# Two sigmoids of a pair of groups placed ahead of the squares of their step, in the other order

## The chip, the cores and the metric

The kernel runs on one core of one Trainium2 chip. The metric is the device time of one execution in microseconds. The core has five engines that run their own instruction streams in order and meet only through semaphores: PE (matrix multiply; its weight loads are listed as PEld), DVE (vector), ACT (activation functions), POOL (GpSimd) and SP, which here only issues DMA transfers. Matmul results land in PSUM banks; everything else lives in SBUF tiles.

## The reference: what is computed

Two layers follow each other on x of shape 4 x 12608 x 128, all in float32.

The first is an attention through 32 inducing vectors. For each of the four batches, the 32 vectors attend to all 12608 tokens (stage A below), and the tokens then attend to the 32 results (stage B below):

```
h = mab(I, x)          # softmax(scale * I x^T) x   : 32 x 128 per batch
y = mab(x, h)          # softmax(scale * x h^T) h   : 12608 x 128 per batch
```

The second is a gated channel mix of each token with its predecessor:

```
xk = mu_k * y + (1 - mu_k) * y_prev
xr = mu_r * y + (1 - mu_r) * y_prev
k  = relu(xk @ w_k)              # 1024 wide
v  = (k * k) @ w_v
out = sigmoid(xr @ w_r) * v
```

## The kernel before, in words

**Groups, units, steps.** The tokens of a batch are cut into 24 groups of 512 tokens and one of 320 (`NG` = 25). A group's 1024 hidden channels are four *units* of 256 channels (`NU` = 4). The main loop (L1047) runs over steps n, one unit per step, 400 units for the four batches, so a step is one quarter of a group.

**What a step does.** At every even n, `up` (L795) issues on PE the up-projection L803 of two units into the two buffers of `ps_a`. Then `square` (L806) turns one unit's result into its square: DVE rectifies it into `k_t` (L813); ACT squares `k_t` into `kh`, rounded to the matmul's input format (L818), and squares `k_t` again in place in full precision (L820); POOL subtracts the two into the rounding rest `kl` (L823). In some steps (`high_vector`, L1016 to L1021) DVE makes `kh` instead (L815); the in-place square on ACT then waits for it, because it overwrites what DVE reads. Four steps later (`LAG` = 4), `down` (L825) multiplies `kh` and `kl` by the split w_v (L831) and accumulates a group's output in one of two PSUM banks `ps_v`. `gate` (L834) multiplies it by the sigmoid `rT`, and `store` transposes it and sends it out on SP's queue.

**The gate's sigmoid.** The matmuls for two groups, 2k and 2k+1, are issued together on PE by `zpair` (L858), at steps n = 8k+6, from k = 1 on: 49 pairs. They are three pairs of matmuls at L781. One group's result goes to the `ps_v` bank that `down` of group 2k+1 will fill two steps later; the other's goes to a bank borrowed from the attention, `pb_a` or `pb_b`. `pb_a` is stage A's bank, for its scores (L372) and its accumulation (L441); `pb_b` is stage B's, for its scores (L620). The borrowed bank becomes free when ACT has read it with the sigmoid (L786), and what the attention issues on PE next into that bank waits for this. `zpair` returns a function that emits the two sigmoids, in the order of the groups: first the one in `ps_v` (the earlier group), then the one in the borrowed bank. The loop calls it after the step's squares. For the last pair of all, `pb_b` takes the place of `ps_v`. Groups 0 and 1 have their sigmoid from `zgate`, which is not touched.

**The attention between.** Stage A of the next batch and stage B of this one are cut into small pieces that are put into the loop at given steps: `at(n, f)` places one at the end of step n, `soon(n, f)` before the squares of step n (the exponentials of both stages, L409 and L637, go there). The exponential and the sigmoid need different activation tables, so ACT loads a table (listed under the line of the instruction that needs it, L786, L408 or L637) whenever it goes from one to the other; the squares, copies and casts need no load.

**Order.** The program is written in the order in which each engine executes it (`manual_schedule`); the semaphore waits follow from which tile is read and written. Nothing is planned from costs. On SP's queue stand, in program order, the transfers of stage A's transposed input (`xt`, L347), of stage B's results into the tiles `R` that the up-projection and the gate read (L587, L600, doubled onto the other half of the partitions by L594), the inputs' loads (L207) and the stores (L854). A buffer of `R` is refilled only after the gate matmuls L781 of the group that used it.

Of the kernel before, what the change touches and what calls it, by code (L numbers as in the profile page):

```python
# [19 lines left out]
def kernel(  # L20
# [46 lines left out]
    def pv_tile(side=None):  # L67

        return pv.tile([P, G], F32, name=f"ps_v{next(sides) if side is None else side % 2}")

    def pb_tile(bank=None):

        return pb.tile([P, G], F32, name="pb_" + (bank or next(banks)))
# [784 lines left out]
    def zpair(n, two):  # L858

        last = two[1].b == B - 1 and two[1].g == NG - 1  # L860
        r = n - (0 if n >= UB else 4)
        spot = r % UB
        side = "b" if r < (B - 1) * UB and SEG <= spot < 7 * SEG and spot % SEG == 2 else "a"
        ps = [pb_tile("b") if last else pv_tile(two[1].b * NG + two[1].g), pb_tile(side)]
        ps = [t[:, :grp.w] for grp, t in zip(two, ps)]
        for m, (a, k) in enumerate(TERMS):
            for h in range(2):
                two[h].zpart(ps[h], a, k, slice(HP * h, HP * (h + 1)), m)
        return lambda: run([lambda grp=grp, t=t: grp.sigmoid(t) for grp, t in zip(two, ps)])

    def run(th):
        for f in th:
            f()
# [68 lines left out]
    def head():  # L942


        last = NBLK - 1
        ab[0].tr()
        warm(8)
        ab[1].tr()
        ab[0].scores()
        for k in range(NBLK):  # L950
            ab[k].maxi()
            ab[k].expo()
            place(PARTS[k][0])
            if k > 0:
                ab[k - 1].hmm()
            if k == last:
                maxes()
            if k > 0:
                ab[k - 1].acc()
                ab[k - 1].sums()  # L960
            if k == 0:
                constants()
            if k + 2 < NBLK:
                ab[k + 2].tr()
            if k == last:
                ab[k].sums()
                weights()
                spin(3)
            ab[k].etrans()
            place(PARTS[k][1])  # L970
            ab[k].ecopy()
            if k < last:
                ab[k + 1].scores()
        gate = weights_sum()
        held = sm.tile([P, 1], F32, name="held", bufs=1)
        nc.gpsimd.tensor_copy(out=held, in_=gate[:, 0:1])
        for c in range(FC // cg):
            split_wv(c)
        spin(3)
        ab[last].hmm()  # L980
        ab[last].acc()
        load_x(1, 0)
        hfin()
        assert not work
# [10 lines left out]
    def start():  # L995

        wk = wpart(0, pv_tile)
        wg = wpart(1, pv_tile)
        (sc0, df0, ex0, nm0, turn0, hi0, lo0, idle), *rest = [stage_b_first(g) for g in range(Q)]
        run([sc0, wk[0], rest[0][0], df0, ex0, wk[1], nm0, lambda: idle(1), turn0, hi0, wk[2], lo0])  # L1000
        plan = ((None, None, None, at, soon, soon, at), (at,) * 4 + (soon, soon, at), (at, at, soon, at, soon, soon, at))
        steps = ((0, 0, 0, 0, 2, 2, 2), (0, 1, 1, 2, 4, 4, 4), (4, 5, 6, 7, 8, 8, 8))
        for fs, when, ns in zip(rest, plan, steps):
            for k, (f, put, n) in enumerate(zip(fs, when, ns)):
                if put is not None:
                    put(n, f)
                elif k > 0:
                    f()
        at(0, wg[0])
        at(0, wg[1])  # L1010
        at(1, wg[2])
        soon(3, lambda: units[0][0].zgate())
        soon(7, lambda: units[NU][0].zgate())
# [3 lines left out]
    for b in range(B):  # L1017
        t = b * UB + (4 if b == 0 else 0)
# [14 lines left out]
    for b in range(B):  # L1033
        for g in range(NG):
            grp = Group(b, g)
# [8 lines left out]
    with tc.manual_schedule():  # L1044
        head()
        start()
        for n in range(len(units) + LAG + 2):  # L1047
            grp, u = units[n] if n < len(units) else (None, n % NU)
            old, ou = units[n - LAG] if LAG <= n < len(units) + LAG else (None, 0)
            for grp_ in gates.pop(n, []):  # L1050
                grp_.gate()
            if grp is None:
                run(late)
                late = []
            else:
                if n % 2 == 0:
                    for g, v in units[n:n + 2]:
                        g.up(v)
                sig = None
                if n % (2 * NU) == NU + 2 and n > 2 * NU:  # L1060
                    sig = zpair(n, (units[n - NU - 2][0], units[n - 2][0]))
                run(early.pop(n, []))
                whole = n in (end - 3, end - 1, end)
                low = grp.square(u, n in high_vector, whole)
                run(late)
                late = [low] if whole else []
                if not whole:
                    low()
                if sig:
                    sig()  # L1070
            for grp_ in stores.pop(n, []):
                grp_.store()
            if old is not None:
                old.down(ou)
            run(events.pop(n, []))
# [30 lines left out]
```

## Time and profile before

| what | value |
|---|---|
| median of 3 runs | 1184.02 us (1182.8 to 1186.4) |
| the profiled execution | 1180.83 us, its span 1179.0 us |
| busy in the span: PE, DVE, ACT, POOL | 92%, 77%, 82%, 80% |
| mean granted clock of PE | 0.983 |
| one square on ACT (L818, L820), mean | 1041 and 1050 ns |
| one sigmoid of 128x512 (L786), mean | 584 ns |
| one activation table load | 1283 ns |
| one subtraction on POOL (L823), mean | 2379 ns |

How to read the lines that follow: a line of the timeline gives the start in us from the beginning of the span, the duration, the engine, the source line, the operation and its tiles, then in brackets how long the engine stood idle before it and what ended that. A line of waits gives who waited for whom, the total in us, how often, and the longest. A busy PE includes modelled ends of its matmuls.

### The profile page before, as it was taken

The numbers are of one execution on the slowest core, as the hardware profiler recorded it, in microseconds if no ns is written. First come the engines' busy times: TensorE is split into PE (matmuls) and PEld (weight loads), VectorE is DVE, ScalarE is ACT, GpSimd is POOL, SyncE is SP. The second block draws the span as 40 slices with busy tenths as digits, with TensorE's granted clock in tenths as the row PEclk, the third lists the DMA queues.
The fourth block names the chain that finished last, engine by engine and source line by source line (L and its number), as shares of the span: only waits on it lengthen the run. The fifth ranks groups of instructions, "written<-read, shape, count | busy, mean of one in ns | idle before, by whom it ended". The sixth has DMA issues, their size and how long they took to land.

```text
span 1179.0 us, 19549 instructions
## 1 busy us (share of the span) xinstructions
PE 1089.9 (92%) x6722; PEld 739.2 (63%) x6722; DVE 904.3 (77%) x1296; ACT 966.5 (82%) x1101; POOL 945.1 (80%) x419
## 2 busy tenths in 40 slices
PE   7799999989999998999999999898989899999998
PEld 5456566656666665666656656556665666666676
DVE  5798788876778887887778788877757677878665
ACT  6497788777898888777989878878678989999996
POOL 2278878878879887777879978877777899999996
PEclk9999999989999999999999999999999999999999
DMA  9215646456155564656326636565422444344431
GB/s 280 89 28 117 154 105 153 99 126 140 29 110 129 126 134 116 143 131 127 61 42 122 151 91 144 117 139 134 83 47 36 89 96 90 63 92 79 81 66 33
DMA packets 267634, 123.61 MB, mean 105 GB/s; under 512 B 225648, under 2 KB 247056, under 8 KB 265232
## 3 DMA queue, kind: packets, MB, share of 16 engines
q1 hardware_dynamic: 267200, 122.35, 47.7%
q8 instruction: 53, 0.87, 0.3%
q14 instruction: 45, 0.37, 0.1%
q10 hardware_dynamic: 336, 0.02, 0.0%
HBM read 28.07 MB, written 25.82 MB: 46 GB/s over the span
## 4 chain that ended last, share of the span: by engine, by line
PE 44%; DVE 21%; ACT 19%; issue 8%; SPq 4%; DMA 3%; DVEq 0%; ACTq 0%
PE ps_v L831 23%; PE ps_a L803 14%; DVE k_t L813 11%; ACT kh L818 5%; ACT k_t L820 5%; ACT rT L786 3%; ACT L786 2%; PE pb_a L372 2%; DVE ot L847 1%; PE pb_b L620 1%; PE pb_a L441 1%; DVE kh L815 1%; SPq L854 1%; DVE oT L836 1%; DMA out_dram<-ot 1%
## 5 line engine op out<-in xcount | busy, mean ns | idle before, releaser
L823 POOL TENSOR_TENSOR kl<-k_t,kh 128x1024 fp32r<-128x1024 f32 (+1 forms) x397 | 933.4, 2379 | 189.5 <-ACT k_t L820 160.7
L813 DVE TENSOR_SCALAR k_t<-ps_a 128x1024 f32<-128x1024 f32 (+1 forms) x400 | 475.1, 1197 | 142.9 <-PE ps_a L803 134.4
L818 ACT ACTIVATE kh<-k_t 128x1024 fp32r<-128x1024 f32 (+1 forms) x352 | 366.3, 1041 | 119.7 <-DVE k_t L813 118.4
L820 ACT ACTIVATE k_t<-k_t 128x1024 f32<-128x1024 f32 (+1 forms) x397 | 416.4, 1050 | 55.9 <-DVE kh L815 23.6
L803 PE MATMUL ps_a<-R,W 64*128 64x512 f32 (+1 forms) x2400 | 343.2, 416 | 7.9 <-DVE k_t L813 6.5
L803 PEld LDWEIGHTS ps_a<-R,W 64*128 64x128 f32 x2400 | 212.9, 189 | 137.9 <-issue 50.0
L831 PE MATMUL ps_v<-kh,wvh 128*128 128x512 f32 (+1 forms) x800 | 273.3, 423 | 8.4 <-ACT rT L786 8.2
L831 PE MATMUL ps_v<-kh,wvl 128*128 128x512 f32 (+1 forms) x800 | 249.1, 393 | 0.0
L831 PE MATMUL ps_v<-kl,wvh 128*128 128x512 f32 (+1 forms) x800 | 248.6, 392 | 0.0
L831 PEld LDWEIGHTS ps_v<-kh,wvh 128*128 128x128 f32 x800 | 134.2, 189 | 102.2 <-issue 62.1
L831 PEld LDWEIGHTS ps_v<-kh,wvl 128*128 128x128 f32 x800 | 150.7, 189 | 35.1
L831 PEld LDWEIGHTS ps_v<-kl,wvh 128*128 128x128 f32 x800 | 149.7, 188 | 34.9
L836 DVE TENSOR_TENSOR oT<-ps_v,rT 128x512 f32<-128x512 f32 (+1 forms) x100 | 66.8, 668 | 6.9 <-PE ps_v L831 6.2
L847 DVE STREAM_TRANSPOSE ot<-oT 128x512 f32<-128x512 f32 x96 | 66.8, 696 | 0.0
L815 DVE SCALAR_TENSOR_TENSOR kh<-ps_a,k_t 128x1024 fp32r<-128x1024 f32 x48 | 58.8, 1225 | 2.5
L344 DVE STREAM_TRANSPOSE xs<-xb 128x512 f32<-128x512 f32 x72 | 50.0, 695 | 0.9 <-issue 0.4
L375 DVE TENSOR_REDUCE mx<-pb_a 128x1 f32<-128x512 f32 x18 | 12.5, 692 | 44.6 <-PE pb_a L372 44.6
L781 PE MATMUL ps_v<-R,Wg 64*128 64x512 f32 (+1 forms) x150 | 45.4, 404 | 0.0
L372 PE MATMUL pb_a<-xt,indT 128*32 128x512 f32 x144 | 26.7, 670 | 18.0 <-ACT rT L786 15.4
L786 ACT ACT_TABLE_LOAD x31 | 39.8, 1283 | 0.6
L781 PE MATMUL pb_a<-R,Wg 64*128 64x512 f32 (+1 forms) x120 | 36.3, 410 | 2.3 <-ACT e1t L409 2.3
L441 PE MATMUL pb_a<-xb,e 128*32 128x128 f32 x576 | 20.2, 282 | 15.7 <-ACT rT L786 15.7
(222 smaller groups left out, 645.4 us busy)
## 6 DMA issues: line engine op xcount, KB each, us to landing
out_dram<-ot SPq DMA_DIRECT2D x184, 128.0 KB, 2.8
R<-R SPq DMA_DIRECT2D x88, 256.0 KB, 3.0
xb<-in_x_dram SPq DMA_DIRECT2D x18, 1024.0 KB, 5.4
xt<-xs SPq DMA_DIRECT2D x288, 64.0 KB, 2.0
R<-hl SPq DMA_DIRECT2D x96, 128.0 KB, 2.3
R<-hl SPq DMA_DIRECT2D x96, 127.8 KB, 2.4
kh<-in_x_dram SPq DMA_DIRECT2D x4, 512.0 KB, 7.7
kl<-in_x_dram SPq DMA_DIRECT2D x4, 512.0 KB, 7.4
```

Of the source, the lines that this page charges most:

```text
L372: nc.tensor.matmul(out=ps[M * i:M * (i + 1), :], lhsT=indT, rhs=S.xt[j, i], start=True, stop=True)
L781: nc.tensor.matmul(out=ps, lhsT=self.S.Wg[a][rows, :], rhs=self.S.R[self.g][rows, k, :self.w], start=(n == 0), stop=(n == len(TERMS) - 1))
L786: nc.scalar.activation(out=self.rT, in_=ps, func=AF.Sigmoid)
L803: nc.tensor.matmul(out=ps[:, r, :w], lhsT=S.W[a][rows, u * P:(u + 1) * P], rhs=R[rows, k, :w], start=(n == 0), stop=(n == 2))
L813: nc.vector.tensor_scalar(out=k, in0=ps, scalar1=0.0, scalar2=None, op0=ALU.max)
L815: nc.vector.scalar_tensor_tensor(out=kh, in0=ps, scalar=0.0, in1=k, op0=ALU.max, op1=ALU.mult)
L818: nc.scalar.activation(out=kh, in_=k, func=AF.Square)
L820: nc.scalar.activation(out=k2, in_=k, func=AF.Square)
L823: return lambda: eng.tensor_tensor(out=kl, in0=k2, in1=kh.bitcast(F32), op=ALU.subtract)
L831: nc.tensor.matmul(out=self.v, lhsT=wt[:, fc, :], rhs=kk[:, c, :], start=(fc == 0 and n == 0), stop=(fc == FC - 1 and n == 2))
L836: nc.vector.tensor_tensor(out=self.oT, in0=self.v, in1=self.rT, op=ALU.mult)
L847: nc.vector.transpose(out=ot[:, o:o + w], in_=self.oT)
```

## The change

Two places are edited. In the loop, the call that emits the two sigmoids moves from behind the step's squares (and behind POOL's subtraction) to in front of them; it stays behind the early pieces, so behind the exponentials of that step. In `zpair`, the two sigmoids swap places: the one in the borrowed bank comes first. The names of the two `rT` buffers swap with them. PE's instructions and their order, DVE's, POOL's and the transfers are as before.

```diff
@@ zpair
-        return lambda: run([lambda grp=grp, t=t: grp.sigmoid(t) for grp, t in zip(two, ps)])
+        return lambda: run([lambda grp=grp, t=t: grp.sigmoid(t) for grp, t in zip(two[::-1], ps[::-1])])
@@ the loop over steps
                 run(early.pop(n, []))
+                if sig:
+                    sig()
                 whole = n in (end - 3, end - 1, end)
                 low = grp.square(u, n in high_vector, whole)
                 run(late)
                 late = [low] if whole else []
                 if not whole:
                     low()
-                if sig:
-                    sig()
```

## The prediction

> **What bounds the kernel now.** I read the page's head first, then who waited for whom, then the timeline around single pair steps, then the DMA queue beside them.
>
> ```profile
> span 1179.0 us, 19549 instructions
> PE 1089.9 (92%) x6722; PEld 739.2 (63%) x6722; DVE 904.3 (77%) x1296; ACT 966.5 (82%) x1101; POOL 945.1 (80%) x419
> ```
> ```profile
> POOL kl L823 <- ACT k_t L820: 160.7, 122, 10.7
> DVE k_t L813 <- PE ps_a L803: 134.4, 90, 6.2
> PEld ps_a L803 <- DVE k_t L813: 20.1, 37, 1.8
> PE pb_a L441 <- ACT rT L786: 15.7, 9, 2.9
> PE pb_a L372 <- ACT rT L786: 15.4, 8, 2.6
> PE ps_v L831 <- ACT rT L786: 8.2, 8, 1.9
> PE pb_b L620 <- ACT rT L786: 8.2, 7, 1.3
> PE pb_a L372 <- DMA R<-R: 2.5, 1, 2.5
> PE pb_a L556 <- ACT rT L786: 2.2, 1, 2.2
> ```
>
> The profiled execution took 1180.83 us, 1.8 outside its span; the median of the runs is 1184.02, 3.2 above it, and I put the change onto that median. PE is the fullest engine, and the others trail it: POOL waits for ACT's squares, DVE's rectifier L813 waits for PE's up-projection L803. PE itself has only 89 us idle, and 49.7 of them (15.7 + 15.4 + 8.2 + 8.2 + 2.2) end with a sigmoid, L786, that was the last reader of a PSUM bank. The wait of 2.5 us put down to a DMA is one more: its weight load names L786. So some 52 us of PE, the engine the others wait for, hang on how late ACT reaches two sigmoids.
>
> **The change, part by part.** No instruction is added or taken away on any engine: 98 sigmoids, their table loads, all DMAs and PE's order stay. On ACT, two sigmoids (with a table load, where an exponential came in between) pass in front of one or two squares, L818 and L820, of their step. What they need, the six L781 matmuls, is issued before that step's squares anyway. The swap inside the pair lets the bank that stage A or B wants go first.
>
> *Stage A's scores, L372, inputs long there.*
>
> ```profile
> 161.48 1.06 ACT L820 ACTIVATE k_t<-k_t 128x1024 f32<-128x1024 f32 x1
> 161.70 0.39 PE L781 MATMUL pb_a<-R,Wg 64*128 64x512 f32 x1
> 164.16 1.06 ACT L820 ACTIVATE k_t<-k_t 128x1024 f32<-128x1024 f32 x1 [1.62 <-DVE kh L815]
> 165.24 1.28 ACT L786 ACT_TABLE_LOAD   x1
> 167.03 0.59 ACT L786 ACTIVATE rT<-pb_a 128x512 f32<-128x512 f32 x1
> 167.67 1.43 PE L372 MATMUL pb_a<-xt,indT 128*32 128x512 f32 x8 [2.58 <-ACT rT L786]
> ```
>
> ACT stood idle 1.62 us before the square. In the new order the load starts when the square of the step before ends, 162.54, and the pb_a sigmoid ends at 162.54 + 1.28 + 0.6 = 164.45; its matmuls ended at 162.09. PE is free at 167.67 - 2.58 = 165.09, so the whole 2.58 goes, with 0.6 to spare. The square itself moves only from 164.16 to about 164.9: most of the 2.4 us that pass it go into ACT's idle time. Four of these sites behave otherwise (next), so of 15.4 + 2.5 there remain 15.4 - 9.5 + 2.5 = **8.4 us**.
>
> *Stage A's scores behind a late transfer.*
>
> ```profile
> 234.17 0.67 SPq L587 DMA_DIRECT2D R<-hl  x1
> 236.25 2.44 SPq L347 DMA_DIRECT2D xt<-xs  x4
> 239.88 0.63 PE L372 MATMUL pb_a<-xt,indT 128*32 128x512 f32 x3 [2.58 <-ACT rT L786]
> 839.90 2.44 SPq L347 DMA_DIRECT2D xt<-xs  x4
> 842.61 1.92 PE L372 MATMUL pb_a<-xt,indT 128*32 128x512 f32 x7 [1.80 <-ACT rT L786]
> ```
> ```profile
> xt<-xs SPq DMA_DIRECT2D x288, 64.0 KB, 2.0
> ```
>
> At four sites (first and last shown; three like the first, 3 x 2.58 + 1.80 = 9.5 us of wait) the last four transfers of xt stand on SP's in-order queue behind L587, which waits for the L781 matmuls of this very step. The fourth is issued near 236.25 + 1.85 = 238.1 and lands 2.0 later, 240.1: at the moment the sigmoid now releases PE. The earlier sigmoid therefore lets three of four score tiles run, and the fourth keeps PE. I take 2.5 us over the four (the fourth tile alone takes about 1.0 from its landing to the next block, against 1.8 from 239.88 now), with 0 and 9.5 as ends.
>
> *Stage A's accumulation, L441.*
>
> ```profile
> 189.46 0.61 ACT L637 ACTIVATE s<-s 128x512 f32<-128x512 f32 x1
> 189.98 1.05 ACT L820 ACTIVATE k_t<-k_t 128x1024 f32<-128x1024 f32 x1
> 192.83 0.59 ACT L786 ACTIVATE rT<-pb_a 128x512 f32<-128x512 f32 x1
> 193.48 1.08 PE L441 MATMUL pb_a<-xb,e 128*32 128x128 f32 x32 [2.01 <-ACT rT L786]
> ```
>
> New: load at 190.07, pb_a done at 190.07 + 1.28 + 0.6 + 0.03 = 191.98, L441 at 192.03 and 1.45 earlier; 0.56 of the wait stays. Nine sites keep at most 9 x 0.56 = 5.0 of 15.7; two have a wait of only 0.3 and keep nothing, two pass two squares: I keep 3.2, gain **12.5** (10.7 to 15.7).
>
> *Stage B's scores, L620.*
>
> ```profile
> 210.94 1.06 ACT L820 ACTIVATE k_t<-k_t 128x1024 f32<-128x1024 f32 x1
> 215.33 0.59 ACT L786 ACTIVATE rT<-pb_b 128x512 f32<-128x512 f32 x1
> 215.97 1.06 PE L620 MATMUL pb_b<-xt,hT 128*32 128x512 f32 x8 [1.35 <-ACT rT L786]
> ```
>
> No load, two squares passed: pb_b is done at 212.0 + 0.6 = 212.6, PE free at 214.62. All seven go: **8.2**; L556 likewise **2.2**. The down-projection L831 waits for the other bank, now second of the two: two squares of 1.06 come behind it and one sigmoid (about 0.5) ahead, 1.6 earlier against a longest wait of 1.9: **7.8** of 8.2 (5 to 8.2).
>
> *PE's clock.*
>
> ```profile
> 167.67 1.43 PE pb_a L372 x8
> 169.10 2.86 PE ps_a L803 x12
> 194.56 1.59 PE ps_a L803 x12
> 203.74 1.12 PE pb_a L372 x8
> ```
> ```profile
> 167.50:171.00 3.50, 3.33 (x18) 2.06 (x20) 0.90 (x2) 2.61 (x4) 1.15 (x2) 0.69 0.00 0
> 193.30:196.80 3.50, 3.32 (x47) 2.49 (x48) 1.24 (x2) 1.07 (x2) 3.41 (x2) 1.00 1.14 208
> ```
>
> After the 2.58 us wait the granted clock is 0.69 over 3.5 us and two blocks take (1.43 - 1.12) + (2.86 - 1.59) = 1.6 us longer; after 2.01 it stayed at 1.00. Such dips stand behind eight of the waits above; five lie at sites whose wait shrinks under 0.6 (167, 444, 693, 792, 867 us), three at the transfer-bound ones. I count 5 x 1.6 = **8.0** (0 to 12.8). The Trainium skill (TensorE: Matmul & The Clock Gate, Part 1: The HAM clock gate) has the clock halved after an idle window of about 3.4 us, free-running; by it, stalls of 2 to 2.9 us need not cost a dip, and the term would be 0 and the time 1146. The row shows the dip after less than a full window, and the row decides.
>
> *What becomes late.* The squares.
>
> ```profile
> 189.63 7.22 POOL L823 TENSOR_TENSOR kl<-k_t,kh 128x1024 fp32r<-128x1024 f32 x3 [1.98 <-PE ps_v L831]
> 199.12 2.42 POOL L823 TENSOR_TENSOR kl<-k_t,kh 128x1024 fp32r<-128x1024 f32 x1 [2.27 <-ACT k_t L820]
> ```
> ```profile
> 1000.00:1100.00 100.00, 98.74 (x539) 68.18 (x540) 84.06 (x102) 92.14 (x98) 94.25 (x40) 1.00 0.41 80
> ```
>
> At the L441 site the square moves from 189.98 to 192.4, and POOL's second subtraction from 192.03 (189.63 + 7.22/3) to 193.4: 1.4 late. POOL's third ends at 198.3 instead of 196.85, still before the 199.12 at which it waits today, and that step's down-projection comes four steps later. So the queue of four steps and POOL's 160.7 us of waiting hide it. Where the cover is thin, in the last batch (window of 1000 us: columns PE, weight load, DVE, ACT, POOL; POOL 94.25 of 100), about 1.1 us of POOL's idle time falls to each pair of 20 us. If it fails there, 13 pairs cost up to 13 x 1.08 = 14; I take 4, nearer to the covered rows.
>
> **Sum:** 8.4 + 2.5 + 12.5 + 8.2 + 2.2 + 7.8 + 8.0 - 4 = **45.6 us**. 1180.8 - 45.6 = 1135.2 for a profiled execution, 1184.0 - 45.6 = **1138** for the median.
>
> **The rivals.** *DVE becomes the bound.* DVE waits for PE 134.4 us, which speaks against; but in the mixed stretches its pieces of both stages lie back to back, and PE catching up eats that slack. Price: each of the 49 pairs brings one wait for L813 of today's mean, 20.1/37 = 0.54 us, 26 us: 1184 - 19 = 1164.
>
> *The transfers are late at the other score sites too*, since SP's queue is tied to PE's gate matmuls: 8.4 and three dips (4.8) are lost: 1151. Against it: at 167 us all transfers had long landed.
>
> *Slower: the squares bind through POOL.*
>
> ```profile
> L786 ACT ACT_TABLE_LOAD x31 | 39.8, 1283 | 0.6
> ```
>
> Each pair's squares come 1.08 us later (two sigmoids), and 1.28 more where a load goes with them, 29 of the 31 loads. If POOL's subtraction sets when k_t buffers come free for L813 and when L831 can run, 49 x 1.08 + 29 x 1.28 = 90 us come in against 50 of gain: 1184 + 40 = 1224. It decides as soon as POOL's lateness outlasts the 2.27 us it waits today before the next step; at 1.4 it doesn't.
>
> *It doesn't do what it says:* PE's waits stay because something else releases PE at the same moment everywhere, as the transfers do at four sites: 1184.
>
> **Chances.** Forecast 0.58, no clock term 0.05, DVE 0.17, transfers 0.06, nothing 0.05, squares 0.09. The forecast's own range is 1119 (upper ends: 3.2 + 7 + 0.4 + 4.8 + 4 = 19.4 us more) to 1163 (lower ends: 1.8 + 2.5 + 2.8 + 8 + 10 = 25.1 less); to hold eight in ten it must reach past DVE's 1164: **1119 to 1166**, leaving out the last two cases. 0.3% is about what a measurement can tell here. Faster 0.58 + 0.05 + 0.17 + 0.06 = 0.86, same 0.05, slower 0.09.
>
> **What would show it.** PE's waits for L786 fall from 49.7 to some 5 to 10 us; L620, L556 and L831 vanish from that list, L441 keeps waits near 0.56 five times. At four sites L372 still has a gap, now with xt transfers as releaser. The granted clock's mean rises from 0.983. POOL's wait for L820 shrinks by roughly the time gained, and its busy time stays. Wrong if new waits PE L803 <- DVE L813 of tens of us appear, if L831 begins to wait for POOL L823, or if the four transfer sites lose their gap altogether.

## The result, and the profile after

The changed kernel takes 1131.12 us (median of 4 runs, 1131.11 to 1134.28). The kernel before, run beside it, took 1183.41 (1182.67 to 1186.4). The ratio is 0.956 with a 95% interval of 0.9537 to 0.9584: 52.3 us less, against 45.6 forecast and a predicted 1138.

The head of the page after:

```profile
span 1129.1 us, 19547 instructions
PE 1083.1 (96%) x6722; PEld 733.4 (65%) x6722; DVE 903.1 (80%) x1296; ACT 963.3 (85%) x1101; POOL 944.8 (84%) x419
```

The profiled execution took 1131.12 us. Its span is 49.9 us shorter than that of the kernel before, and PE's two parts of it are: its idle time fell from 1179.0 - 1089.9 = 89.1 to 1129.1 - 1083.1 = 46.0 us (43.1 less), and its busy time by 6.8. PE's and DVE's instructions come in the same order as before; only ACT's order differs, with the same 31 table loads.

The list of waits after, those that answer to the lines shown of before (who waited for whom, total in us, times, longest):

```profile
POOL kl L823 <- ACT k_t L820: 120.6, 108, 10.7
DVE k_t L813 <- PE ps_a L803: 98.3, 86, 3.3
DVE k_t L813 <- POOL kl L823: 8.0, 11, 2.4
PE ps_a L803 <- DVE k_t L813: 7.9, 14, 1.4
PE pb_a L352 <- ACT e1t L409: 7.8, 3, 2.8
PE pb_a L441 <- ACT rT L786: 3.1, 6, 0.6
PE pb_a L372 <- DMA xt<-xs: 2.3, 2, 1.2
PE pb_a L372 <- ACT k_t L820: 2.0, 2, 1.0
PE ps_v L831 <- ACT rT L786: 0.6, 1, 0.6
```

Of 52.2 us of PE waiting that ended with a sigmoid L786 (the 2.5 put down to a DMA counted in), 3.1 + 0.6 = 3.7 are left, and the mean granted clock rose from 0.983 to 0.995. L620 and L556 are gone from the list. The two lines for L372 are new: the four score sites with a late transfer. Two of the four are put down to the square L820; the experiment on the transfers below shows that it is not what they wait for. POOL's wait for the square fell by 40 us while its busy time stayed, so POOL's slack is what paid for the time gained.

The site at 167 us before, now 5 us earlier (timeline, with ACT, PE and POOL):

```profile
158.80 1.06 ACT L820 ACTIVATE k_t<-k_t 128x1024 f32<-128x1024 f32 x1
159.88 1.28 ACT L786 ACT_TABLE_LOAD   x1
161.18 0.60 ACT L786 ACTIVATE rT<-pb_a 128x512 f32<-128x512 f32 x1
161.67 0.59 ACT L786 ACTIVATE rT<-ps_v 128x512 f32<-128x512 f32 x1
162.15 1.06 ACT L820 ACTIVATE k_t<-k_t 128x1024 f32<-128x1024 f32 x1
162.36 1.07 PE L372 MATMUL pb_a<-xt,indT 128*32 128x512 f32 x8
163.28 2.41 POOL L823 TENSOR_TENSOR kl<-k_t,kh 128x1024 fp32r<-128x1024 f32 x1 [0.33 <-ACT k_t L820]
```

Table load and both sigmoids now stand in front of the square. L372 starts without a gap and takes 1.07 us instead of 1.43. The square runs beside it, and POOL waits 0.33 us for it.

The site at 240 us before, now with the transfer as its limit (PE, ACT and SP's queue):

```profile
226.12 0.60 ACT L786 ACTIVATE rT<-pb_a 128x512 f32<-128x512 f32 x1
226.32 2.44 SPq L347 DMA_DIRECT2D xt<-xs  x4
228.38 2.91 PE L372 MATMUL pb_a<-xt,indT 128*32 128x512 f32 x8 [1.02 <-DMA xt<-xs]
231.22 1.67 PE L803 MATMUL ps_a<-R,W 64*128 64x512 f32 x12
```

The bank is free at 226.12 + 0.60 = 226.72, PE has nothing else to do from 228.38 - 1.02 = 227.36, and still it stands until 228.38. Then the block takes 2.91 us instead of some 1.07; that further parts of xt land only while it runs is tested below. Such a stretched block counts as busy, so the 4.3 us in the list of waits are not all that these transfers cost. Two more blocks are stretched with no gap in front of them: 2.47 us at 266.97 and 2.22 us at 426.05.

### The profile page after: what moved, and what is told of

Its sections match the earlier page's. It is cut to its first block, busy times and chain, and to the rows that moved or that the text cites. A ratio compares the mean times of both kernels' runs of the same rounds, so it can differ in the third digit from the quotient of the medians.

```text
span 1129.1 us, 19547 instructions
## 1 busy us (share of the span) xinstructions
PE 1083.1 (96%) x6722; PEld 733.4 (65%) x6722; DVE 903.1 (80%) x1296; ACT 963.3 (85%) x1101; POOL 944.8 (84%) x419
## 4 chain that ended last, share of the span: by engine, by line
PE 64%; DVE 14%; ACT 11%; issue 4%; SPq 3%; DMA 2%; POOL 1%; DVEq 0%; ACTq 0%; POOLq 0%
PE ps_v L831 35%; PE ps_a L803 20%; DVE k_t L813 7%; ACT kh L818 3%; ACT k_t L820 3%; PE pb_a L372 3%; PE ps_v L781 2%; PE pb_b L620 1%; PE pb_a L441 1%; ACT L786 1%; DVE oT L836 1%; DVE xs L344 1%; DVE ot L847 1%; SPq L100 1%; SPq L193 1%
## 5 line engine op out<-in xcount | busy, mean ns | idle before, releaser
L823 POOL TENSOR_TENSOR kl<-k_t,kh 128x1024 fp32r<-128x1024 f32 (+1 forms) x397 | 933.2, 2385 | 140.0 <-ACT k_t L820 120.6
L813 DVE TENSOR_SCALAR k_t<-ps_a 128x1024 f32<-128x1024 f32 (+1 forms) x400 | 475.7, 1197 | 108.4 <-PE ps_a L803 98.3
L820 ACT ACTIVATE k_t<-k_t 128x1024 f32<-128x1024 f32 (+1 forms) x397 | 415.7, 1050 | 37.9 <-DVE kh L815 5.6
L803 PE MATMUL ps_a<-R,W 64*128 64x512 f32 (+1 forms) x2400 | 337.6, 410 | 9.5 <-DVE k_t L813 7.9
L803 PEld LDWEIGHTS ps_a<-R,W 64*128 64x128 f32 x2400 | 209.1, 186 | 135.5 <-issue 49.2
L831 PE MATMUL ps_v<-kh,wvh 128*128 128x512 f32 (+1 forms) x800 | 272.0, 422 | 0.6 <-ACT rT L786 0.6
L831 PE MATMUL ps_v<-kh,wvl 128*128 128x512 f32 (+1 forms) x800 | 249.0, 393 | 0.0
L831 PE MATMUL ps_v<-kl,wvh 128*128 128x512 f32 (+1 forms) x800 | 248.6, 392 | 0.0
L831 PEld LDWEIGHTS ps_v<-kh,wvh 128*128 128x128 f32 x800 | 133.6, 189 | 92.4 <-issue 58.1
L831 PEld LDWEIGHTS ps_v<-kh,wvl 128*128 128x128 f32 x800 | 150.2, 189 | 34.7
L831 PEld LDWEIGHTS ps_v<-kl,wvh 128*128 128x128 f32 x800 | 149.8, 188 | 34.9 <-POOL kl L823 0.2
L375 DVE TENSOR_REDUCE mx<-pb_a 128x1 f32<-128x512 f32 x18 | 12.5, 692 | 32.9 <-PE pb_a L372 32.9
L372 PE MATMUL pb_a<-xt,indT 128*32 128x512 f32 x144 | 29.1, 604 | 4.2 <-DMA xt<-xs 2.3
L781 PEld LDWEIGHTS ps_v<-R,Wg 64*128 64x128 f32 x150 | 27.8, 190 | 5.9 <-issue 0.5
```

The source lines that it names most:

```text
L372: nc.tensor.matmul(out=ps[M * i:M * (i + 1), :], lhsT=indT, rhs=S.xt[j, i], start=True, stop=True)
L781: nc.tensor.matmul(out=ps, lhsT=self.S.Wg[a][rows, :], rhs=self.S.R[self.g][rows, k, :self.w], start=(n == 0), stop=(n == len(TERMS) - 1))
L803: nc.tensor.matmul(out=ps[:, r, :w], lhsT=S.W[a][rows, u * P:(u + 1) * P], rhs=R[rows, k, :w], start=(n == 0), stop=(n == 2))
L813: nc.vector.tensor_scalar(out=k, in0=ps, scalar1=0.0, scalar2=None, op0=ALU.max)
L820: nc.scalar.activation(out=k2, in_=k, func=AF.Square)
L823: return lambda: eng.tensor_tensor(out=kl, in0=k2, in1=kh.bitcast(F32), op=ALU.subtract)
```

## The experiments

Each ratio is to runs of the kernel before on the same chip. The two halves of the change, the earlier transfers in the kernel after and the late squares ran beside one set of them (median 1185.88); the earlier transfers in the kernel before, the last batch and the first filling beside another (1184.54); the second filling beside a third (1185.09).

**Which half of the change carries it.** First the moved call with the old order inside the pair, as an edit of the kernel after:

```diff
-        return lambda: run([lambda grp=grp, t=t: grp.sigmoid(t) for grp, t in zip(two[::-1], ps[::-1])])
+        return lambda: run([lambda grp=grp, t=t: grp.sigmoid(t) for grp, t in zip(two, ps)])
```

> The changed kernel (1131.1 us) with the old order inside the pair: both sigmoids ahead of the squares, the one in ps_v first. My theory (PE waits for banks, ACT's place in the order sets how long): the borrowed bank is read one sigmoid, about 0.5 us, later. L372 at sites without a late transfer has 0.6 us to spare and stays free; the five waits of L441 go from 0.56 to about 1.06, two others grow by up to 0.5, so PE's waits of L441 rise from 3.1 to about 6.5 us, and the time to 1134 to 1135. Rival, the order inside the pair carries much of the gain: 1145 or more. Rival, it carries nothing: 1131.

Measured: 1136.32 us, ratio 0.9597 (0.9565 to 0.9629), 1 to 2 us more than expected; PE's wait at L441 is 6.6 us, as expected. Then the swap inside the pair alone, as an edit of the kernel before (the same two lines, the other way round):

> The kernel before (1183.4 us) with only the order inside the pair changed; the sigmoids stay behind the squares. My theory: the borrowed bank comes free 0.5 us earlier, so L372, L441 and L620 win about 0.5 us at each of 25 waits (12 us), the waits of L831 for the other bank grow by 0.5 us each (4 us at eight sites, some new ones), and some clock dips go as waits fall from 2.6 to 2.1 us (up to 5 us): 1170 to 1177. Rival, the order carries much of the gain: 1160 or less. Rival, nothing: 1183.

Measured: 1173.63 us, ratio 0.9904 (0.9872 to 0.9936), as expected. The position carries some 49.6 us and the order alone 12.3 (1185.88 less each). Together they are not 62 but 52, since both shorten the same waits: with the position changed, only some 5 us are left for the order. The intervals of the two ratios, 0.956 and 0.9597, overlap by a little; the order's share on top of the position rests as much on the trace, where L441 waits 3.1 us instead of 6.6. The list of waits with the order alone shows what it trades:

```profile
PE ps_v L831 <- ACT rT L786: 12.8, 10, 2.4
PE pb_a L441 <- ACT rT L786: 12.8, 9, 2.4
PE pb_a L372 <- ACT rT L786: 11.7, 6, 2.1
PE pb_b L620 <- ACT rT L786: 4.8, 7, 0.9
```

Each attention bank comes about half a microsecond earlier, and the down-projection's bank that much later: L831 waits 12.8 us instead of 8.2.

**Whether the transfers are the limit at the four sites.** In the kernel after, stage A's last transposition is placed one step earlier, so that its four transfers go onto SP's queue ahead of L587:

```diff
-            at(t + ((1, 2, 3, 7) if b > 1 or j > 1 else (-1, 0, 1, 3) if j else (4, 5, 6, 7))[c], lambda c=c: btr(c))
+            at(t + ((1, 2, 3, 6) if b > 1 or j > 1 else (-1, 0, 1, 3) if j else (4, 5, 6, 7))[c], lambda c=c: btr(c))
```

> The changed kernel with the last of stage A's four transposes one step earlier (7 becomes 6 in its list of steps), so that its four transfers of xt stand on SP's queue ahead of the refill that waits for the gate matmuls. My theory (at four sites L372 now waits for these transfers: its block takes 2.9 us from a start that is already 1.0 late, against 1.07): about 2.8 us come back at each of the four and 1 to 1.4 us at two more whose block takes 2.2 and 2.5 us, so 10 to 14 us: 1117 to 1121, and L372 blocks of 1.07 everywhere. Rival, the gap there is caused by ACT (one view names the square L820 as releaser): 1131.

Measured: 1117.44 us (1116.5 to 1119.06), ratio 0.9436 (0.9406 to 0.9466), as expected. This beats both kernels. SP's queue and PE at the same site:

```profile
220.67 3.07 SPq L347 DMA_DIRECT2D xt<-xs  x4
224.57 0.63 SPq L587 DMA_DIRECT2D R<-hl  x1
227.62 1.07 PE L372 MATMUL pb_a<-xt,indT 128*32 128x512 f32 x8
```

The transfers now stand ahead of L587 and no longer wait for the gate matmuls with it. The groups of instructions (busy us, mean ns of one, idle us before) give the price, first after, then with this edit:

```profile
L372 PE MATMUL pb_a<-xt,indT 128*32 128x512 f32 x144 | 29.1, 604 | 4.2 <-DMA xt<-xs 2.3 <-ACT k_t L820 2.0
```
```profile
L372 PE MATMUL pb_a<-xt,indT 128*32 128x512 f32 x144 | 19.2, 605 | 0.0
```

4.2 us of waiting and 9.9 of stretched blocks go, 14.1 in all: at the four sites with a gap, and some 2.5 of it at the two stretched blocks without one. All 18 blocks now take 1.07 us. The time falls by 1131.1 - 1117.4 = 13.7 between the medians, which were taken in different sets of runs, and by 12.0 between the two profiled spans, since PE waits 2.5 us more at L803 and L534 there.

The same edit in the kernel before:

> The kernel before (1183.4 us) with only the last of stage A's four transposes one step earlier (7 becomes 6). My theory: at the four sites the sigmoid ends at about the moment the last transfer lands, so removing the transfer alone gains only what it keeps inside the block of L372 (0.4 to 0.9 us at four or five sites): 1180 to 1183. If the transfers had been the cause of those waits before, 4 x 2.5 us and their clock dips would go: 1168 or less.

Measured: 1185.97 us over 10 runs, ratio 1.0012 (0.9998 to 1.0026): not even the little that was expected. There L372 still waits for the sigmoid, and the long block is now the clock's doing, which was 0.50 from 239.78 on:

```profile
239.91 2.25 PE L372 MATMUL pb_a<-xt,indT 128*32 128x512 f32 x8 [2.56 <-ACT rT L786]
```

So some 12 to 14 us hang on the transfers only once the sigmoid is early. Taking one of two limits away that end together brings nothing; that is why the transfers did not show in the waits of before.

**What late squares cost.** In the kernel after, two more sigmoids of the same size, whose results nobody reads, come behind the real two and ahead of the squares. Nothing of the computation is left out.

```diff
+        def both():
+            for grp, t in zip(two[::-1], ps[::-1]):
+                grp.sigmoid(t)
+            for grp in two[::-1]:
+                junk = mp.tile([P, G], F32, name="junk", bufs=1)[:, :grp.w]
+                nc.scalar.activation(out=junk, in_=grp.rT, func=AF.Sigmoid)
+        return both
```

> The changed kernel with two more sigmoids of the same size behind each pair's two, from rT into a tile nobody reads: the banks come free as early as before, but the squares of each of the 49 pair steps come about 1.08 us later still. My theory (PE sets the pace, POOL's waiting and the four steps between squares and down-projection hide late squares): between 0 and 10 us, 1131 to 1141, most of it in the last batch. Rival, squares bind through POOL: 49 x 1.08 = 53 us, 1184.

Measured: 1147.39 us, ratio 0.9695 (0.9659 to 0.9732): 16 us more than after, outside what my theory gave and far under the 53 of the rival. Waits that grew:

```profile
POOL kl L823 <- ACT k_t L820: 147.4, 102, 10.7
DVE k_t L813 <- POOL kl L823: 40.0, 43, 3.5
PE ps_a L803 <- DVE k_t L813: 11.9, 15, 2.0
```

The chain that the slower rival described does exist: a late square makes POOL late (147.4 instead of 120.6), POOL holds `k_t` buffers that DVE's L813 needs (40.0 instead of 8.0, 43 times instead of 11), and PE waits more for DVE. It is not shown to be the whole price. PE's idle time grew by 11.7 us, from 46.0 to 57.7; 4.0 of them stand in the last line and 1.1 in new waits of L831 for POOL, and the rest is spread over small waits. The added sigmoids also give ACT 50 us more to do (1013.6 us busy instead of 963.3), and this run does not part that from the lateness. Together they cost 16 of the 49 x 1.08 = 53 us that were added. The change itself adds no work to ACT and stays inside the cover; a second delay of the same size, with its work, does not.

The change for the last batch alone, where I had feared for the cover, is the other side of it. It is an edit of the kernel before: the pairs of steps from 300 on are swapped and emitted ahead of the squares.

```diff
+        o = -1 if n >= 3 * UB else 1
+        return lambda: run([lambda grp=grp, t=t: grp.sigmoid(t) for grp, t in zip(two[::o], ps[::o])])
...
+                if sig and n >= 3 * UB:
+                    sig()
+                    sig = None
```

> The kernel before with the change made only for the pairs of the last batch (steps from 300 on), where no stage A runs and POOL is 94% busy. It separates the price of late squares where the cover is thinnest (prediction: 4 us, at most 14) from the waits of L831 that go there (4.3 us in five waits). My theory: 1179 to 1184, gain and price nearly cancel. Rival, late squares bind through POOL there: 1190 or more. Rival, they cost nothing: 1179.

Measured: 1180.63 us over 10 runs, ratio 0.9964 (0.9951 to 0.9976), so 2.8 to 5.8 us faster. PE's waits at L831 behind 860 us, before and here:

```profile
PE ps_v L831 <- ACT rT L786: 4.3, 5, 1.9
```
```profile
PE ps_v L831 <- ACT rT L786: 1.5, 2, 1.3
```

2.8 us of waiting go, and no price is to be seen. The window of 890 to 1170 us (PE, weight load, DVE, ACT, POOL, clock), before and here:

```profile
890.00:1170.00 280.00, 273.11 (x1501) 190.22 (x1498) 210.28 (x247) 254.90 (x275) 261.32 (x112) 1.00 0.38 73
```
```profile
890.00:1170.00 280.00, 275.84 (x1519) 192.09 (x1518) 212.83 (x251) 256.73 (x278) 263.73 (x113) 1.00 0.39 75
```

PE does 18 matmuls more in the same stretch, and POOL, with 263.73 of 280 us busy, still leaves 16.

**The clock.** In the kernel before, six matmuls into a buffer of `ps_a`, whose results nobody reads, are put ahead of L372 at the seven sites that wait longest for a sigmoid. They take up time in which PE stood; nothing of the computation is left out.

```diff
         def scores():
+            if t % 8 == 4 and j > 0:
+                spin(6)
```

> The kernel before with six matmuls of 128x512 that write into a free ps_a buffer and that nobody reads, put ahead of stage A's scores L372 at the seven sites behind a pair step (not the first of each batch). They work about 1.4 us inside waits of 1.8 to 2.6 us. My theory of the clock term (a wait of 2 us or more at these sites halves the granted clock for a while): the waits of PE and the block order stay, the dips at 167, 239, 444, 515, 693 and 765 us go, and 5 to 9 us with them: 1174 to 1178, mean clock about 0.99. If the dips cost nothing on the path, or aren't caused by the waits: 1183.

Measured: 1182.36 us over 10 runs, ratio 0.9984 (0.9972 to 0.9996), so 0.5 to 3.3 us. My theory had said 1174 to 1178. The windows of 7 us (columns as above) at the first filled site and at the next L441, which was not filled, first before, then with the fill:

```profile
167.00:174.00 7.00, 6.33 (x28) 4.08 (x29) 3.80 (x6) 4.96 (x7) 3.31 (x2) 0.76 0.00 0
193.00:200.00 7.00, 6.52 (x64) 4.84 (x66) 4.37 (x8) 4.39 (x5) 4.64 (x3) 1.00 0.97 183
```
```profile
167.00:174.00 7.00, 5.80 (x33) 3.58 (x32) 3.35 (x6) 5.79 (x7) 4.70 (x3) 1.00 0.21 31
193.00:200.00 7.00, 6.24 (x53) 4.63 (x54) 3.07 (x6) 3.31 (x5) 4.00 (x2) 0.76 1.03 193
```

The dip left the filled site and came back at the wait of 2 us that had none before. Read through the whole trace in windows of 3.4 us, start and end left out, 11 dips became 12. So filling these waits alone left as many dips as before. The last kernel also fills the seven L441 sites that wait 2 us or more:

```diff
             if half == 0:
+                if (b, j) in ((1, 0), (1, 2), (2, 0), (2, 2), (3, 1), (3, 3), (3, 5)):
+                    spin(6)
```

> The kernel before, with six matmuls of 128x512 whose results nobody reads put ahead of L372 at the seven pair sites and also ahead of L441 at the seven sites that wait 2.0 us or more for a sigmoid (121, 193, 397, 469, 720, 792 and 868 us). Nothing of the computation is left out; the matmuls only fill time in which PE waited for a sigmoid. The sigmoids, the squares and every wait's end stay where they were, so what changes is whether PE stands still long enough for a dip of the granted clock. Theory (a dip of 1.6 us needs an uninterrupted wait of 2 us or more, and which of the waits gets it is a matter of phase): with both groups of waits filled, dips remain only behind the waits for L409 at L352 and in the end of the kernel, about 3 to 4 instead of 11 and 12, and the time falls by 8 x 1.55 = 12 us to about 1172 (1168 to 1176), less where a fill of six matmuls outlasts its wait. Rival (dips come on a grid of their own whatever PE does, or their cost lies in time that PE would wait anyway): as many dips and 1181 to 1185 us.

Measured: 1172.75 us (1170.13 to 1177.58), ratio 0.9906 (0.9878 to 0.9933), 12.3 us less, as expected, though the edit moves nothing on ACT and PE has 84 matmuls more to do. The window around the L441 whose wait was 2.01, and its first line (this kernel's lines stand 4 further down: L445 is L441, L835 is L831, L790 is L786):

```profile
192.50:198.50 6.00, 6.00 (x52) 4.30 (x42) 4.45 (x8) 3.39 (x4) 3.67 (x3) 1.00 0.85 165
191.89 1.08 PE L445 MATMUL pb_a<-xb,e 128*32 128x128 f32 x32 [0.64 <-ACT rT L790]
```

L441 starts at 191.89 instead of 193.48, 1.59 us earlier. L372 before it was already 0.11 earlier (167.56 instead of 167.67), so 1.5 us are the price of the one dip between them. The count of dips came out higher than I had written, which was 3 to 4: the profiled execution (1176.12 us, the second slowest of six, with a clock of 0.987) still has seven of them outside the start and the end, some behind waits of 1.51 to 1.87 us:

```profile
354.65 0.91 PE L835 MATMUL ps_v<-kh,wvh 128*128 128x512 f32 x2 [1.51 <-ACT rT L790]
930.97 0.73 PE L835 MATMUL ps_v<-kh,wvh 128*128 128x512 f32 x2 [1.87 <-ACT rT L790]
```

## Why the prediction was right

The median came out at 1131.1, inside the range and 7 us under the forecast. The terms against the two profiled executions (span less 49.9), each from the list of waits or the groups:

| term | forecast us | measured us | from |
|---|---|---|---|
| L441 | 12.5 | 12.6 | waits 15.7 to 3.1 |
| L620, L556 | 8.2 + 2.2 | 8.2 + 2.2 | both gone |
| L831 | 7.8 | 7.6 | 8.2 to 0.6 |
| L372, both kinds of site | 8.4 + 2.5 | 11.4 | idle 18.0 to 4.2, busy 26.7 to 29.1 |
| clock | 8.0 | 9.2 | fall of PE's busy time without L372: 6.8 + 2.4 |
| late squares | -4 | about -1.6 | L803's idle time 7.9 to 9.5 |
| sum | 45.6 | 49.6 | 49.9 in the span |

That the measured column comes to the span is bookkeeping, since PE's idle and busy time make up the span; the test is row by row.

The groups L803 and L372 (busy us, mean ns, idle us before), before, and L803 after:

```profile
L803 PE MATMUL ps_a<-R,W 64*128 64x512 f32 (+1 forms) x2400 | 343.2, 416 | 7.9 <-DVE k_t L813 6.5 <-ACT R L748 0.7 <-DVE kh L815 0.3
L372 PE MATMUL pb_a<-xt,indT 128*32 128x512 f32 x144 | 26.7, 670 | 18.0 <-ACT rT L786 15.4 <-DMA R<-R 2.5
```
```profile
L803 PE MATMUL ps_a<-R,W 64*128 64x512 f32 (+1 forms) x2400 | 337.6, 410 | 9.5 <-DVE k_t L813 7.9 <-ACT R L748 0.7 <-DVE kh L815 0.6
```

Most of the clock's gain is in L803, whose 2400 matmuls take 5.6 us less, since it is what PE does behind most of these waits.

*The waits* went as worked out from single sites; those that end with a sigmoid came to 3.7 us, a little under the 5 to 10 that I had named. At L441 the remaining wait was put at 0.56 for a passed square and a table load, and 3.2 in all:

```profile
184.95 1.08 PE L441 MATMUL pb_a<-xb,e 128*32 128x128 f32 x32 [0.56 <-ACT rT L786]
```

Five such waits and one of 0.30 make 3.1.

*The transfer-bound sites* behaved as the step said: at four sites the gap stays, and xt ends it. Gap and block together took 18.2 us there before and take 15.9 now, so 2.3 us were gained where 2.5 were forecast. What I had not seen are the two other sites whose blocks are stretched; all these late transfers together cost some 12 to 14 us after the change. The rival that the transfers are late at all score sites is out: at 12 of 18, that at 162.36 us among them, L372 runs without a gap and in 1.07 us.

*The clock* was the term with the widest bounds, 0 to 12.8. Dips outside the start and the end fell from 11 to 3. My count, five gone at the sites whose wait shrinks below 0.6 and three staying at the transfer-bound sites, was off: those went too, and their unbroken stall is now 1.2 us at most. The price was off the other way: eight dips gone for 9.2 us are 1.15 us each, against 1.6, or 1.35 with the 1.6 us by which L372's blocks at 167 and 694 us got shorter (1.43 and 2.33 to 1.07 each), which the table has under L372. That 5 x 1.6 came so near is luck. The kernel that fills most of the long waits bears out that dips cost time: 12.3 us, and 1.5 at the one dip shown. The rule of the Trainium skill that I weighed (TensorE: Matmul & The Clock Gate, Part 1) asks for an idle window of about 3.4 us; here dips followed waits of 1.51 to 2.9 us, so the measurement decides against waits of that length being needed. That the place of a dip is a matter of phase (the 2.01 us wait had none, until the dip before it was taken away) agrees with its free-running window.

*The late squares* were the term that was mis-sized: 4 taken, some 1.6 found, if all that L803 waits longer is put down to them, and none to be seen in the last batch, where I had put it. The reasoning on the queue of four steps held. What I had not said is how little is left of it: another 1.08 us of ACT per pair costs 16.

*DVE as the bound* did not come: PE's wait for L813 rose by 1.4 us, not 26, and DVE still waits 98.3 us for PE.

The difference of 52.3 in the medians to 49.7 between the profiled executions is the kernel before: its profiled run was 2.6 us under the median. It had a clock of 0.983, the 25 runs of the second set have a median of 0.981, and a straight line through their clocks and times gives 0.76 us for 0.001; by this estimate the clock explains 1.5 of the 2.6.

## What to carry to other kernels

When an engine that is nearly full waits for a short instruction on another engine, look at what that other engine does first and whether anybody waits for it: two sigmoids of 0.6 us behind two squares of 1.06 cost 4% here, since the squares had four steps of room and the sigmoids none. Before such a wait is removed, ask what else ends at the same moment: a transfer that costs nothing today (1.0012 when moved alone) was worth 14 us afterwards. And ask how much of the cover the change uses up, since the next delay of the same size may be paid for.

## What the runs showed of the hardware

A wait of PE costs more than its length when a dip of the granted clock follows: some 1.5 us on top at the one dip that could be followed alone, and 1.2 us on average between the profiled executions before and with both kinds of wait filled (four dips fewer, 4.7 us). The dips did not belong to places: filling the waits of one kind moved them to the waits of the other kind, with no fewer of them (11 and 12) and 0.16% of the time gained; filling both gained 0.9%. Why the average lies under 1.5 is not shown; a later wait may take part of it up. The lines through clock and time of the kernel before are too loose to tell: 0.76 us for 0.001 over 25 runs, 0.97 over 7, 1.69 over 11, which at 1.7 us of clock per dip (half a clock over 3.4 us, 0.0014 of the span) would be 1.1, 1.4 or 2.4 us.

No length of wait parted those with a dip from those without: one of 1.51 us had one, one of 2.01 us had none. What parts most of them is how a wait lies on a grid. The dips of a trace begin whole multiples of 3.413 us apart (before: 168.86, 240.54 and 261.02 us, which is 21 and 6 steps). Windows of one step, first around the wait ahead of 167.67 and the one ahead of 193.48 in the kernel before, then around the latter with the L372 waits filled (columns as in the windows above; the clock is the third number from the end):

```profile
165.45:168.86 3.41, 1.19 (x8) 0.47 (x8) 0.36 (x1) 3.40 (x5) 2.48 (x2) 1.00 0.27 28
168.86:172.27 3.41, 3.41 (x15) 2.21 (x14) 2.12 (x3) 1.47 (x3) 1.99 (x1) 0.50 0.00 0
189.34:192.75 3.41, 2.12 (x10) 1.37 (x8) 3.31 (x5) 3.38 (x5) 3.12 (x2) 1.00 0.87 178
192.75:196.17 3.42, 2.69 (x45) 1.95 (x45) 0.71 (x2) 1.62 (x3) 3.33 (x2) 1.00 1.19 206
```
```profile
190.82:194.23 3.41, 1.39 (x22) 0.86 (x25) 2.20 (x4) 3.38 (x5) 3.41 (x2) 1.00 0.99 190
194.23:197.65 3.42, 3.42 (x36) 2.43 (x26) 0.66 (x1) 0.42 (x1) 2.77 (x2) 0.50 1.16 208
```

PE stood for 2.22 us of the first step, and the next has half the clock. The wait of 2.01 us was cut in two by a border, 1.29 and 0.73 us, and had no dip; with the fill the same wait fell into one step, 2.02 us, and had one. In the kernel before, the steps ahead of ten of its eleven dips had PE idle for 2.0 us or more and the eleventh for 1.67; no step without a dip behind it, the first 5 us aside, had more than 1.79. This is read from the traces and not tested by an edit, and it has an exception: with the order alone, a step with 2.01 us idle had no dip.

The matmul group with partly landed inputs hid 9.9 us of stalls in its busy time (29.1 against 19.2 us); the list of waits showed 4.2.
